# Weight and moving tiles of the second network's matmuls: 64 bytes longer, begun at offsets of 0 to 56 bytes in turn

## The chip, the cores and the metric

The kernel runs on one core of a Trainium2 chip. The metric is the time of one execution on the device in microseconds, the median of repeated runs. TensorE (PE) multiplies a stationary operand (the weights, loaded by a weight load, PEld) with a moving operand that streams past it; VectorE (DVE) and ScalarE (ACT) prepare operands; SyncE (SP) issues the DMAs. All operands of the matmuls lie in the on-chip memory SBUF, which has 128 partitions; a byte address below is the address inside a partition.

## What is computed

An attention between eight blocks of 512 tokens and 32 state rows each, then two feed-forward networks of the same shape, one with a squared ReLU and one with an ELU:

```python
def _moe_ref(x, w_in, w_out):          # 4608 tokens, 512 -> 2048 -> 512
    h = x @ w_in
    r = np.maximum(h, 0.0)
    g = r * r
    return (g @ w_out).astype(np.float32)

def _moe2_ref(x, w_in, w_out):
    h = x @ w_in
    g = np.where(h > 0.0, h, np.exp(np.minimum(h, 0.0)) - 1.0)
    return (g @ w_out).astype(np.float32)

attn_out = _attn_ref(**attn_kwargs)
x = np.ascontiguousarray(attn_out.transpose(0, 2, 1, 3)).reshape(B * S, H * D)
x = _moe_ref(x=x, **moe_kwargs)
return _moe2_ref(x=x, **moe2_kwargs)
```

## The kernel before

Every float32 value is split into a rounded high part and the rest (HI and LO, both of type float32r), and a product of two values is made of three matmuls: HI by LO, HI by HI, LO by HI. `split` makes the two parts: ACT copies the value into HI (L163), DVE subtracts HI from the value and writes LO (L164).

The program has three stretches. In the first (to about 560 us of the span) attention and the first network run block by block; its matmuls are `h<-at,m` and `acc<-gs,v` (L158 to L160), and conversions of the weights of both networks run beside them. In the second (560 to about 687 us) the last two blocks go as a pair. In the third (687 us to the end) the second network runs: four pairs of blocks, one after the other, and then the state rows. A pair is treated as a 2 by 2 block matrix, and the product of two such matrices is made of seven products instead of eight, with sums and differences of the operands as inputs.

In a pair of the second network, `first_product` runs 7 products for each of 8 column groups j, and `second_product` (by way of `out_products`) again 7 products of 8 pieces. Each product of one piece takes one weight tile `wr` (HI and LO, 2 by 256 float32, 2,048 bytes in a partition) and is six matmuls of 512 columns, all on line L43. The moving operand is a tile `xf` (in the first product: HI and LO of 2 by 512 values, 8,192 bytes) or `gp` (in the second: HI and LO of two pieces, 8,192 bytes). `wr` tiles come from HBM by one DMA each (L753), through 12 buffers; `xf` tiles (7 buffers) and `gp` tiles (3 buffers) are written by `split`. Four pairs, two products, 56 pieces, six matmuls: 2,688 matmuls of 512 columns. The state rows follow with 192 matmuls `hs<-xs,pl` and 192 `as<-gss,pl` of 256 columns, whose weights `pl` lie in buffers of the pool `xf`.

Instructions are put into their engines' queues in the order in which the program is written; the background work (`x_forms`, which makes the next pair's `xf`) is called from `second_product` at fixed steps.

Where tiles start is set by the pools, which are laid out one after the other. In the built program of the kernel before, the weight slice and the moving slice of each of the 2,688 and 384 matmuls start at multiples of 64 bytes, and for each matmul the two starts leave the same remainder when divided by 512 (128 and 128, say). The same holds for `acc<-gs,v` and for `x`, `y`, `z<-gp,wr` of the pair of the first network (448 and 448). It does not hold for `h<-at,m`: there the moving slice `at` leaves 448 and the weight slice `m` leaves 128. `h<-at,m` and `X<-xf,wr` are otherwise alike: six matmuls of 512 columns into one bank, in the same order of HI and LO.

Of the kernel before, what the change touches and what calls it, by code (L numbers as in the profile page):

```python
# [10 lines left out]
F32R = mybir.dt.float32r  # L11
# [6 lines left out]
B, H, S, NS, D = 8, 8, 512, 32, 64  # L18
DM, DFF = 512, 2048
P = 128  # L20
# [8 lines left out]
RAW, CV = 4, 4  # L29
NF = 7  # L30
HF = FC // 2

CLAMP = 2.0 ** -96 * (2.0 - 2.0 ** -3 - 2.0 ** -22)
SIGN = -(1 << 31)
# [4 lines left out]
def product(nc, ps, w, x, last, start):  # L39

    for k, (wk, xk) in enumerate(zip(w, x)):
        for i, (a, b) in enumerate(((HI, LO), (HI, HI), (LO, HI))):
            nc.tensor.matmul(ps, wk[a], xk[b], start=start and k == 0 and i == 0,  # L43
                             stop=last and k == len(w) - 1 and i == 2, skip_group_check=True)


def out_products(nc, split, g, weight, unit, step, put, sbuf, psum):


    gp_p, eu_p, u2_p, oo_p = sbuf  # L50
    tt, act = nc.vector.tensor_tensor, nc.scalar.activation
    count = iter(range(NF * HF))

    def phase(f, src, ps, start, combine=None):
        for j in range(HF):
            jj, r = divmod(j, 2)
            if combine and r == 0:
                combine(jj)
            if r % unit == 0:
                t = gp_p.tile([P, 2, unit, S], F32R, name="gp", tag="gp")  # L60
                split(t[:, HI], t[:, LO], src[jj][:, r:r + unit])
            w = weight(j, f)
            for m in range(2):
                sl = slice(m * P, (m + 1) * P)
                product(nc, ps[m], [(w[:, HI, sl], w[:, LO, sl])], [(t[:, HI, r % unit], t[:, LO, r % unit])],
                        j == HF - 1, start and j == 0)
            step(next(count))

    def copied(ps, p, name):
        t = p.tile([P, S], F32, name=name, tag=name)  # L70
        act(out=t, in_=ps, func=AF.Copy)  # L71
        return t

    def added(e, half, ps, u):
        for m in range(2):
            o = oo_p.tile([P, S], F32, name="o", tag="o")
            tt(out=o, in0=ps[m], in1=u[m], op=ALU.add)
            put(e, 2 * half + m, o)

    def sub(out, a, b):  # L80
        return lambda jj: tt(out=out[jj], in0=a[jj], in1=b[jj], op=ALU.subtract)

    a11, a12, a21, a22 = (g[q] for q in (11, 12, 21, 22))
    x, y, z = [[p.tile([P, S], F32, name=c, tag=c) for _ in range(2)] for p, c in zip(psum, "xyz")]
    phase(1, a11, x, True)
    p1 = [copied(t, eu_p, "eu") for t in x]
    phase(2, a12, y, True)
    added(0, 0, y, p1)
    phase(6, a11, x, False, sub(a11, a21, a11))
    u2 = [copied(t, u2_p, "u2") for t in x]  # L90
    phase(5, a21, z, True)
    phase(7, a21, x, False, sub(a21, a22, a11))
    u3 = [copied(t, eu_p, "eu") for t in x]
    added(1, 1, z, u3)
    phase(4, a22, x, False)
    for m in range(2):
        o = oo_p.tile([P, S], F32, name="o", tag="o")
        act(out=o, in_=x[m], func=AF.Copy)
        put(1, m, o)
    phase(3, a12, z, False, sub(a12, a12, a11))  # L100
    added(0, 1, z, u2)
# [3 lines left out]
def attn_mlp_kernel(ctx: ExitStack, tc: tile.TileContext, xt, xn, st, w1, v1, w2, v2, outx, outs):  # L105
# [16 lines left out]
    def pools(stack):  # L122
        return lambda name, bufs, **kw: stack.enter_context(tc.tile_pool(name=name, bufs=bufs, reuse_waits="tile", **kw))

    pool = pools(one)
# [16 lines left out]
    pool = pools(single)  # L142
# [19 lines left out]
    def split(hi, lo, src):  # L162
        copy = nc.scalar.activation(out=hi, in_=src, func=AF.Copy)  # L163
        nc.vector.tensor_tensor(out=lo, in0=src, in1=hi.bitcast(F32), op=ALU.subtract)  # L164
        return copy
# [3 lines left out]
    if True:  # L169
# [30 lines left out]
        def convert(name, i, out):  # L200

            t = raw.pop((name, i))
            low, high = t[:, :, 0], t[:, :, 1]
            bits = out.bitcast(I32)
            after = pace if name in ("w2", "v2") else gate
            with tc.issue_after(after[0].ins) if after else nullcontext():
                nc.scalar.activation(out=out, in_=high.bitcast(F32), func=AF.Copy, scale=2.0 ** -112)  # L210
            with tc.issue_after(gate[0].ins) if gate else nullcontext():
                nc.scalar.activation(out=low, in_=low.bitcast(U32), func=AF.Copy, scale=2.0 ** -29)
            yield
            nc.vector.tensor_scalar(out=out, in0=out, scalar1=CLAMP, scalar2=-CLAMP, op0=ALU.min, op1=ALU.max)
            nc.vector.tensor_single_scalar(out=bits, in_=bits, scalar=3, op=ALU.logical_shift_left)
            yield
            nc.vector.tensor_tensor(out=bits, in0=bits, in1=low, op=ALU.add)
            yield
            nc.vector.scalar_tensor_tensor(out=bits, in0=high, scalar=SIGN, in1=bits, op0=ALU.bitwise_and, op1=ALU.bitwise_or)
# [45 lines left out]
        def conv_pair(name, j):  # L265


            v = [conv_p["cv"].tile([P, 512], F32, name="cv", tag="cv") for _ in range(2)]
            for _ in zip_longest(convert(name, j, v[0]), convert(name, j + HF, v[1])):
                yield  # L270
# [9 lines left out]
        def sums_v1(j):  # L280

            v = [conv_p["cv"].tile([P, 512], F32, name="cv", tag="cv") for _ in range(2)]
            for r in range(2):
                f = j + r * HF
                nc.sync.dma_start(out=v[r], in_=wd["v1", f])
# [11 lines left out]
        for i in range(16):  # L297
            pieces += [("v1", i)] + ([("w1", i + 4)] if i < 12 else [])
        pairs2 = [(name, j) for name in ("w2", "v2") for j in range(HF)]
        converting = pieces + [("f1", j) for j in range(HF)] + pairs2  # L300
# [303 lines left out]
        pool = pools(double)  # L604
# [86 lines left out]
        for i in range(FC + LAG):  # L691
            if i < FC:
# [6 lines left out]
                t = gs[i] = gp1_p.tile([P, 2, NST], F32R, name="gs", tag="gp")  # L699
# [4 lines left out]
            f = i - LAG  # L704
# [4 lines left out]
            w, t = v1s.pop(f), gs.pop(f)  # L709
# [16 lines left out]
    xf_p = pool2("xf", NF)  # L726
    wr_p = pool2("wr", 12)
# [3 lines left out]
    gp_p = pool2("gp", 3)  # L731
# [14 lines left out]
    def copied(ps, p=None, name="eu"):  # L746
        t = (p or eu_p).tile([P, S], F32, name=name, tag=name)
        act(out=t, in_=ps, func=AF.Copy)  # L748
        return t

    def weight(name, j, f):
        t = wr_p.tile([P, 2, 256], F32R, name="wr", tag="wr")
        nc.sync.dma_start(out=t.bitcast(F32), in_=wf[name, j][:, f - 1])  # L753
        return t

    xf, xr = {}, {}
# [5 lines left out]
    def x_forms(n):  # L762

        t1, t2 = xr[2 * n], xr[2 * n + 1]
        a11, a12, a21, a22 = t1[:, DM1], t1[:, DM2], t2[:, DM1], t2[:, DM2]

        def put(f, src):
            t = xf[n, f] = xf_p.tile([P, 2, 2, S], F32R, name=f"xf{n}_{f}", tag="xf")
            split(t[:, HI], t[:, LO], src)

        put(1, a11)
        yield
        put(2, a12)
        yield
        tt(out=a21, in0=a21, in1=a22, op=ALU.add)
        put(5, a21)
        yield
        tt(out=a11, in0=a21, in1=a11, op=ALU.subtract)
        put(6, a11)
        yield  # L780
        tt(out=a21, in0=a22, in1=a11, op=ALU.subtract)
        put(7, a21)
        yield
        put(4, a22)
        yield
        tt(out=a12, in0=a12, in1=a11, op=ALU.subtract)
        put(3, a12)
        yield

    def first_product(n, g):  # L790
# [6 lines left out]
        def prod(f, ps, j, start):  # L797
            w, x = weight("w2", j, f), xf[n, f]
            ws = [(w[:, HI, k * P:(k + 1) * P], w[:, LO, k * P:(k + 1) * P]) for k in range(2)]
            product(nc, ps, ws, [(x[:, HI, k], x[:, LO, k]) for k in range(2)], True, start)  # L800
# [41 lines left out]
    def second_product(n, g, bg):  # L842
        def step(i):
            if i % HF == 3:
                next(bg, None)

        def put(e, k, o):
            nc.sync.dma_start(out=outx[k * P:(k + 1) * P, (2 * n + e) * S:(2 * n + e + 1) * S], in_=o)

        out_products(nc, split, g, lambda j, f: weight("v2", j, f), 2, step, put, (gp_p, eu_p, u2_p, oo_p),  # L850
                     (ps_x, ps_y, ps_z))


    plain = {}
# [3 lines left out]
        nc.sync.dma_start(out=t, in_=wd[name, j])  # L858

    def split_plain(name, j):  # L860
        t = xf_p.tile([P, 2, 2, 512], F32R, name="pl", tag="xf")
        split(t[:, HI], t[:, LO], plain[name, j])
        plain[name, j] = t

# [19 lines left out]
    def state_block(prepared):  # L884
# [5 lines left out]
        def refill():  # L890
            x = next(nxt, None)
            if x:
                split_plain(*x)
            x = next(ahead, None)
            if x:
                load_plain(*x)
# [94 lines left out]
```

## Time and profile before

| | |
|---|---|
| times of the two runs shown | 1352.22 and 1353.41 us, median 1352.82 |
| span of the profiled execution (first to last instruction) | 1350.5 us |
| what lies around the span, by the median | 2.3 us |
| PE busy | 98% of the span, 7,064 matmuls |
| granted TensorE clock, mean | 0.997 |
| third stretch, the four pairs | 687 to 1300 us of the span |
| third stretch, state rows | 1300 us to the end |

The profile gives no time of its own for the profiled execution beside its span. The page's busy shares count each engine's instructions; matmuls are pipelined, so that a matmul's listed length (390 ns) is longer than the distance from its start to the next one's. The pace of PE is read from the chain that ended last, whose pieces are cut where the next one starts: a piece "x48" of 10.88 us is 48 matmuls at 226.7 ns each.

### The profile page before, as it was taken

What the parts mean: (1) busy time and instruction counts of PE and PEld (TensorE: products, weight loads), DVE (VectorE), ACT (ScalarE), POOL (GpSimd) and SP (SyncE); (2) the same over time, 40 slices, a digit from 0 to 9 for tenths busy, and PEclk for the clock granted to TensorE, in tenths of its full rate; (3) what the DMA queues carried; (4) which work ended last, traced back from release to release, by engine and by line L of the source; (5) the groups of instructions that cost most, each with busy time, mean ns of one, the idle gap of its engine ahead of it and who ended that gap; (6) DMA issues with size and microseconds to landing.
All of it is one profiled execution on the core that took longest, in us unless ns stands there. A gap on an engine that the chain in (4) does not pass through costs nothing.

```text
span 1350.5 us, 19746 instructions
## 1 busy us (share of the span) xinstructions
PE 1327.5 (98%) x7064; PEld 1057.1 (78%) x7064; DVE 951.0 (70%) x1437; ACT 839.5 (62%) x1417; POOL 0.7 (0%) x6
## 2 busy tenths in 40 slices
PE   8989999999999999999999999999999999999998
PEld 6656777777777776778988888888888888888898
DVE  6997868686878865775576884579636884568644
ACT  5887758676777657644467843676446743666444
POOL 0000000000000000000000000000000000000000
PEclk9999999999999999999999999999999999999999
DMA  6988856575857424279077777767776777778732
GB/s 240 318 300 310 305 178 230 201 267 190 279 197 266 151 82 153 97 255 349 25 252 208 224 240 224 208 194 247 229 225 194 206 210 223 209 204 284 226 110 100
DMA packets 127729, 290.72 MB, mean 215 GB/s; under 512 B 13840, under 2 KB 22032, under 8 KB 124560
## 3 DMA queue, kind: packets, MB, share of 16 engines
q1 hardware_dynamic: 127632, 289.46, 66.3%
q8 instruction: 56, 0.92, 0.3%
q14 instruction: 41, 0.34, 0.1%
HBM read 212.86 MB, written 76.55 MB: 214 GB/s over the span
## 4 chain that ended last, share of the span: by engine, by line
PE 89%; DMA 5%; DVE 3%; ACT 3%; issue 1%; SPq 0%; ACTq 0%; DVEq 0%
PE x L43 16%; PE X L43 13%; PE z L43 8%; PE Z L43 6%; PE acc L158 6%; PE acc L159 6%; PE acc L160 6%; PE h L158 5%; PE h L159 4%; PE h L160 4%; PE y L43 4%; PE Y L43 3%; DMA raw_v<-in_v_dram 2%; PE mp L331 2%; PE hs L43 2%; PE as L43 2%
## 5 line engine op out<-in xcount | busy, mean ns | idle before, releaser
L163 ACT ACTIVATE gp<-g 128x1024 fp32r<-128x1024 f32 (+1 forms) x168 | 154.0, 917 | 146.0 <-PE x L43 69.5
L164 DVE TENSOR_TENSOR gp<-g,gp 128x1024 fp32r<-128x1024 f32 (+1 forms) x168 | 174.9, 1045 | 95.4 <-ACT gp L163 94.4
L43 PE MATMUL x<-gp,wr 128*128 128x512 f32 x960 | 223.5, 390 | 0.0
L43 PEld LDWEIGHTS x<-gp,wr 128*128 128x128 f32 x960 | 179.7, 188 | 39.4 <-ACT eu L71 1.9
L43 PE MATMUL X<-xf,wr 128*128 128x512 f32 x768 | 186.7, 390 | 0.0
L43 PEld LDWEIGHTS X<-xf,wr 128*128 128x128 f32 x768 | 143.4, 188 | 31.7 <-ACT u L748 1.3
L158 PE MATMUL acc<-gs,v 128*128 128x512 f32 x384 | 154.4, 402 | 3.8 <-DVE gs L474 1.9
L159 PE MATMUL acc<-gs,v 128*128 128x512 f32 x384 | 150.4, 392 | 0.0
L160 PE MATMUL acc<-gs,v 128*128 128x512 f32 x384 | 150.2, 392 | 0.0
L43 PE MATMUL z<-gp,wr 128*128 128x512 f32 x480 | 110.4, 389 | 0.0
L744 DVE SCALAR_TENSOR_TENSOR g<-r,g 128x512 f32<-128x512 f32 x96 | 63.9, 689 | 65.8 <-ACT r L743 65.8
L43 PEld LDWEIGHTS z<-gp,wr 128*128 128x128 f32 x480 | 90.1, 188 | 18.7
L158 PE MATMUL h<-at,m 128*128 128x512 f32 x256 | 103.0, 403 | 1.7 <-ACT r L469 1.7
L158 PEld LDWEIGHTS acc<-gs,v 128*128 128x128 f32 x384 | 72.0, 188 | 38.1 <-issue 15.9
L160 PE MATMUL h<-at,m 128*128 128x512 f32 x256 | 100.7, 395 | 0.5 <-ACT m L346 0.5
L159 PE MATMUL h<-at,m 128*128 128x512 f32 x256 | 101.0, 395 | 0.0
L43 PE MATMUL Z<-xf,wr 128*128 128x512 f32 x384 | 97.4, 389 | 0.0
L469 ACT ACTIVATE r<-h 128x512 f32<-128x512 f32 x96 | 57.1, 595 | 64.4 <-PE h L160 64.1
L742 ACT ACTIVATE r<-g 128x512 f32<-128x512 f32 x96 | 57.5, 625 | 57.5 <-DVE g L821 40.4
L160 PEld LDWEIGHTS acc<-gs,v 128*128 128x128 f32 x384 | 72.1, 188 | 19.8 <-issue 4.2
L159 PEld LDWEIGHTS acc<-gs,v 128*128 128x128 f32 x384 | 72.2, 188 | 18.6 <-issue 3.4
L43 PEld LDWEIGHTS Z<-xf,wr 128*128 128x128 f32 x384 | 72.1, 188 | 15.0
(145 smaller groups left out, 2173.6 us busy)
## 6 DMA issues: line engine op xcount, KB each, us to landing
wr<-f_v SPq DMA_DIRECT2D x256, 256.0 KB, 3.0
wr<-f_w SPq DMA_DIRECT2D x224, 256.0 KB, 2.9
f_v<-wf SPq DMA_DIRECT2D x40, 512.0 KB, 3.3
raw_w<-in_w_dram SPq DMA_DIRECT2D x32, 512.0 KB, 4.8
raw_v<-in_v_dram SPq DMA_DIRECT2D x32, 512.0 KB, 5.0
f_w<-wf SPq DMA_DIRECT2D x24, 512.0 KB, 2.8
xt<-in_xt_dram SPq DMA_DIRECT2D x8, 1024.0 KB, 6.9
xn<-in_xn_dram SPq DMA_DIRECT2D x8, 1024.0 KB, 6.1
```

What stands on the lines that cost most here:

```text
L43: nc.tensor.matmul(ps, wk[a], xk[b], start=start and k == 0 and i == 0, stop=last and k == len(w) - 1 and i == 2, skip_group_check=True)
L158: mm(ps, w[HI], x[LO], start=first, stop=False)
L159: mm(ps, w[HI], x[HI], start=False, stop=False)
L160: mm(ps, w[LO], x[HI], start=False, stop=last)
L163: copy = nc.scalar.activation(out=hi, in_=src, func=AF.Copy)
L164: nc.vector.tensor_tensor(out=lo, in0=src, in1=hi.bitcast(F32), op=ALU.subtract)
L331: mm(ps[e][32 * k:32 * k + 32, :], st_t[b][r, k, :], x(k, r), start=True, stop=True)
L469: pace[:] = [nc.scalar.activation(out=r, in_=ps, func=AF.Relu)]
L742: act(out=r, in_=h, func=AF.Relu, scale=-1.0)
L744: nc.vector.scalar_tensor_tensor(out=out, in0=r, scalar=-1.0, in1=h, op0=ALU.add, op1=ALU.max)
```

## The change

A new function `shifted` makes a tile that is 16 float32 (64 bytes) longer in each partition and returns a view of it that starts `shift` values after the tile's start. Weight tiles `wr` of the second network take their shifts in turn from a list of nine (0, 8, 16, 24, 32, 40, 48, 56 and 4 bytes), tiles `pl` of the state rows from the same list. Moving tiles `xf` and `gp` of the second network take theirs from a list of five (0, 32, 8, 16 and 48 bytes). `gp` of the first network's pair (where `unit` is 1), its weights (`weight1`) and everything before 687 us stay as they are.

```diff
+PAD = 16
+WSHIFT = (0, 2, 4, 6, 8, 10, 12, 14, 1)
+XSHIFT = (0, 8, 2, 4, 12)
...
+def shifted(pool, name, rows, shift):
+
+    n = rows[0] * rows[1] * rows[2]
+    t = pool.tile([P, n + PAD], F32R, name=name, tag=name)
+    return t[:, shift:shift + n].rearrange("p (a b c) -> p a b c", a=rows[0], b=rows[1])
...
-    count = iter(range(NF * HF))
+    count, turn = iter(range(NF * HF)), iter(range(NF * HF))
...
             if r % unit == 0:
-                t = gp_p.tile([P, 2, unit, S], F32R, name="gp", tag="gp")
+                if unit == 1:
+                    t = gp_p.tile([P, 2, unit, S], F32R, name="gp", tag="gp")
+                else:
+                    t = shifted(gp_p, "gp", (2, unit, S), XSHIFT[next(turn) % len(XSHIFT)])
...
+    wturn = iter(range(B * NF * HF))
+
     def weight(name, j, f):
-        t = wr_p.tile([P, 2, 256], F32R, name="wr", tag="wr")
+        t = shifted(wr_p, "wr", (2, 1, 256), WSHIFT[next(wturn) % len(WSHIFT)])[:, :, 0]
         nc.sync.dma_start(out=t.bitcast(F32), in_=wf[name, j][:, f - 1])
...
-            t = xf[n, f] = xf_p.tile([P, 2, 2, S], F32R, name=f"xf{n}_{f}", tag="xf")
+            t = xf[n, f] = shifted(xf_p, "xf", (2, 2, S), XSHIFT[(f + 3 * n) % len(XSHIFT)])
...
-        t = xf_p.tile([P, 2, 2, 512], F32R, name="pl", tag="xf")
+        t = shifted(xf_p, "xf", (2, 2, 512), WSHIFT[len(plain) % len(WSHIFT)])
```

No instruction is added, removed or moved: PE's 6,434, DVE's 1,439, ACT's 1,403 and SP's 867 rows stand in the same order, with the same waits, in the two built programs. Only addresses differ, and the names (`pl` is now called `xf`). Of the 3,072 matmuls of the third stretch, the two starts leave the same remainder by 512 in 42, lie a multiple of 64 bytes apart in 306 and a multiple of 16 bytes apart in 1,230. 1,800 have a weight slice that does not start at a multiple of 16 bytes, and 576 a moving slice that does not; every moving slice starts at a multiple of 8 bytes.

## Rows read from the trace of the kernel before

**Rows 1.** The page: busy us (share) and count of each engine; clock in 40 slices.
```profile
PE 1327.5 (98%) x7064; PEld 1057.1 (78%) x7064; DVE 951.0 (70%) x1437; ACT 839.5 (62%) x1417; POOL 0.7 (0%) x6
...
PEclk9999999999999999999999999999999999999999
```

**Rows 2.** The page, chain that ended last, shares of the span by engine.
```profile
PE 89%; DMA 5%; DVE 3%; ACT 3%; issue 1%; SPq 0%; ACTq 0%; DVEq 0%
```

**Rows 3.** The chain in order of time (first row: second stretch): start us, us, what.
```profile
606.76 10.88 PE x L43 x48
...
775.82 10.88 PE y L43 x48
786.70 10.88 PE x L43 x48
...
845.48 4.08 PE X L43 x18
...
1317.39 2.88 PE hs L43 x24
1320.27 2.88 PE as L43 x24
```

**Rows 4.** The same chain, 526 to 532 us: h, first and last of 22.
```profile
527.07 0.23 PE h L160
...
531.88 0.23 PE h L160
```

**Rows 5.** Stretch 527.07 to 531.88 us: busy us of each engine, clock, DMA share, GB/s.
```profile
527.07:531.88 4.81, 4.81 (x22) 3.78 (x21) 1.98 (x3) 3.42 (x7) 0.00 (x0) 1.00 0.00 0
```

**Rows 6.** The same view, a pair's first product and its second; columns PE, PEld, DVE, ACT, POOL.
```profile
841.30:920.50 79.20, 79.20 (x350) 65.24 (x349) 53.46 (x71) 55.29 (x93) 0.00 (x0) 1.00 0.70 199
920.50:994.20 73.70, 73.69 (x326) 60.70 (x325) 51.22 (x48) 33.96 (x39) 0.00 (x0) 1.00 0.80 243
```

**Rows 7.** Groups by line and shape, 841.3 to 994.2 us: busy us, mean ns | idle before.
```profile
L43 PEld LDWEIGHTS X<-xf,wr 128*128 128x128 f32 x193 | 36.1, 188 | 7.9 <-ACT u L748 0.3 <-ACT eu L748 0.2
L43 PEld LDWEIGHTS x<-gp,wr 128*128 128x128 f32 x192 | 36.0, 188 | 7.9 <-ACT eu L71 0.4
L164 DVE TENSOR_TENSOR gp<-g,gp 128x1024 fp32r<-128x1024 f32 x28 | 34.2, 1223 | 18.4 <-ACT gp L163 18.2
...
L81 DVE TENSOR_TENSOR g<-g,g 128x1024 f32<-128x1024 f32 x12 | 14.6, 1220 | 0.1
...
L163 ACT ACTIVATE gp<-g 128x1024 fp32r<-128x1024 f32 x28 | 29.7, 1059 | 28.5 <-PE x L43 16.0 <-PE z L43 7.3 <-PE y L43 4.0
```

**Rows 8.** Waits of SP's queue, 841.3 to 994.2 us: total us, times, longest.
```profile
SPq L753 <- PE X L43: 30.9, 31, 2.0
SPq L753 <- PE x L43: 23.2, 27, 1.0
```

**Rows 9.** The page, DMA issues: count, KB each, us from issue to landing.
```profile
wr<-f_v SPq DMA_DIRECT2D x256, 256.0 KB, 3.0
wr<-f_w SPq DMA_DIRECT2D x224, 256.0 KB, 2.9
```

## The prediction

> **What bounds the kernel now.** I read the page's first lines, then the chain that ended last, then the stretches. PE is busy 98% of the span and the granted clock is full throughout, its 2.4 GHz level [rows 1]; 89% of the chain is PE [rows 2]. In the third stretch, the only one whose addresses change, the chain is an unbroken row of matmuls at one pace: 48 in 10.88 us and 18 in 4.08 us, 226.7 ns each for 512 columns, and 24 in 2.88 us, 120.0 ns each for 256 columns [rows 3]. The 2,688 matmuls of the four pairs at 226.7 ns are 609.3 us of the 613 us from 687 to 1300. So nothing matters there but this pace: a nanosecond on each of the 2,688 + 384 = 3,072 matmuls is 3.07 us, 0.23% of the time.
>
> What the pace is made of: 512 columns at 2.4 GHz are 213.3 ns and 256 are 106.7 ns, so each matmul has 13.3 ns on top, whatever its length. All these matmuls have their weight and moving starts in step (the same remainder by 512). The one kind that is out of step is h, with starts 320 bytes apart by that measure: from 527.07 to 531.88 us 21 matmuls of 512 columns take 4.81 us, 229.0 ns each [rows 4]. This is 2.4 ns slower, at full clock, with the DMA engines idle [rows 5], and with six matmuls per bank in the same order of HI and LO as X. What is left to tell h from X is where its operands lie. That is one case, and other differences (two writers of the weights instead of a DMA) are not excluded.
>
> **The change part by part.** Order and waits are the same, so the sum has only terms of duration.
>
> 1. The matmul's pace. 42 of 3,072 matmuls stay in step, 3,030 do not. If being out of step costs what it costs in h, that is 3,030 x 2.4 ns = 7.2 us. The bounds: below, the 13.3 ns on top could be something that starts in step bring about; out of step it could shrink to nothing, 3,072 x 13.3 ns = 41 us less. Nothing excludes that, but h, the only row out of step, went the other way. In between lies zero: the pace doesn't care. Above: see the weight loads. I take h's price, as the nearest row, +7.2 us.
>
> 2. The weight loads. One lasts 188 ns and hides beside the running matmul, which leaves 226.7 - 188 = 38.7 ns of slack; the 7.9 us idle before 193 loads are the 41 ns between them [rows 7]. No row shows a load or a matmul whose operand starts off a multiple of 64 bytes. 1,800 of the weight slices will start off a multiple of 16. A load up to 20% longer stays hidden and costs nothing; beyond that each further nanosecond costs 1.8 us. Taken at nothing, with the upper end kept for a rival. For the 576 moving slices off 16 bytes, the same: nothing, or at the far end as much again as the 13.3 ns that a matmul now has on top, 7.7 us.
>
> [...]
>
> 3. The writers of the moving tiles. In a pair's second product ACT is busy 34.0 us and DVE 51.2 us of 73.7 [rows 6]; a `gp` tile takes ACT 1,059 and DVE 1,223 ns [rows 7] and serves 12 matmuls, 2.72 us. If unaligned writes made DVE's share of a tile 10% longer, 0.12 us, it would still be hidden by the three buffers. Nothing. Without that cover (in a phase that combines, a subtraction of 1,220 ns joins the 1,223 ns [rows 7], 2.44 us of work in 2.72) a DVE pace 15% worse would start to show.
>
> 4. The weight DMAs. A tile of 256 KB is needed every 6 x 226.7 ns = 1.36 us, 193 GB/s. A DMA lands 3 us after its issue [rows 9], and 12 buffers reach 16 us ahead; SP waits for PE to free a buffer, not the other way [rows 8]. The DMA engines are 70% busy in a first and 80% in a second product [rows 6]. Unaligned destinations are in no row. Until the packets take 1.25 times as long (1 / 0.80), it costs nothing; I take nothing. Filling the pipe once at 687 us may take some tenths of a microsecond more.
>
> Sum: 7.2 us on the profiled execution's span, 1350.5 to 1357.7 us. 2.3 us lie around the span by the median and don't change, so 1352.8 becomes 1360.0 us, 0.5% slower.
>
> **The rivals.**
>
> *The pace doesn't care where operands start.* Then all of it falls away: 1352.8 us. For it: the pace in rows 3 is the same at remainders of 128 and, in the first network's pair (the piece at 606.76 us), of 448. Against it: h. [...]
>
> *In-step starts are what costs the 13.3 ns.* The running matmul's reads and the next weights' reads could fall on the same part of the memory at the same moments just because all starts are in step; spreading them would then free it. If half of the 13.3 ns goes, 20 us: 1332 us; all of it, 1312 us. For it: the surplus is the same for 256 and 512 columns, as a cost of each weight load would be. Against it: h has other starts and is slower, and a surplus so constant looks like a fixed part of changing weights.
>
> *Unaligned weight slices load slower than they can be hidden* (the other side, beyond the forecast). From 227 ns (now 188) the next matmul waits for its weights. At +30% a load takes 244 ns, 18 ns over the present pace for 1,800 matmuls, 32 us: with the 7 us of the forecast 1392 us. At +50%, 282 ns, 100 us: about 1453 us. For it: the loads are the closest to a limit of all that changes, with 17% of each matmul's time as slack. Against it: nothing but that a pipelined read of 512 bytes has little reason to grow by a third.
>
> *Unaligned DMA destinations bind.* If packets took twice as long, the wr share of the second product's DMA work (56 x 256 KB = 14.7 of some 17.9 MB, 82%) would add 0.66 to 0.80, and a second product would take 1.46 x 73.7 = 107 us, a first one about as long: 60 us more a pair, 1600 us. It decides from 1.25 times. Against it: count and size of the transfers stay the same.
>
> *The change doesn't do what it says*: the built program shows that it does, so no chance is kept for this.
>
> **How the numbers follow.** Chances: h's price, or up to twice it, 0.40; no difference 0.29; starts in step were the cost 0.10 (half of it beyond 2%); slow weight loads, or a moving slice's, 0.15 (0.13 beyond 2%); DMA 0.06. A measurement of this kernel can tell about 2% from no change, 27 us: faster 0.05, slower 0.19, same 0.76. The forecast is 1360 us. The range goes from 1346 (6.7 us below no difference, a third of the half gain of the second rival) to 1392 (a load 30% longer); it leaves out some 0.07 below and 0.12 above.
>
> **What the profile of the changed kernel would show.** The chain's pieces of 48 matmuls: 10.88 us if nothing matters, about 11.0 if h's price holds, 10.3 or less if in-step starts were the cost. If only the slow weight loads bind, the means of the PEld groups on L46 (L43 before) rise above 227 ns and PE waits; if DMAs bind, SP no longer waits for PE at the weight DMA and PE waits for `wr`. ACT and DVE means for `gp` and `xf` should stay at 1,059 and 1,223 ns. The stretch up to 687 us should not move at all. I would be most wrong if a single shift, such as the 4 bytes of every ninth weight tile or the 8 bytes of every fifth moving tile, had a price of a whole different order: then a few of the matmuls would be very slow and the rest unchanged.

## The result and the profile after

The changed kernel takes 1368.41 us (1368.09 to 1368.74) where the kernel before takes 1352.82: a ratio of 1.0111, 95% interval 1.0081 to 1.0140. It is slower, by 15.6 us, inside the forecast range and on the forecast side; the forecast itself, 1360.0, took half of the loss.

The page of the changed kernel, its span and its engines' busy time:

```profile
span 1366.3 us, 19746 instructions
...
PE 1342.0 (98%) x7064; PEld 1057.2 (77%) x7064; DVE 952.5 (70%) x1437; ACT 839.8 (61%) x1417; POOL 0.7 (0%) x6
```

Beside [rows 1], PE is busier by 14.5 us; the weight loads, DVE and ACT are within 1.5 us of where they were. The chain in order of time (start us, us, what; the first row is of the second stretch, whose addresses did not change):

```profile
609.16 10.88 PE x L46 x48
...
779.90 11.20 PE y L46 x48
791.10 11.16 PE x L46 x48
...
1007.60 4.19 PE X L46 x18
...
1333.73 2.86 PE hs L46 x24
```

The first row has the pace of [rows 3], 226.7 ns a matmul, but starts 2.40 us later. In the pairs of the third stretch 48 matmuls take 11.16 to 11.20 us and 18 take 4.19: 232.5 to 233.3 ns, 5.9 to 6.7 more than before. In the state rows, 24 matmuls of 256 columns take 2.86 us in place of 2.88: they are faster.

Three marks in the chains of both kernels divide the loss: the first piece of 18 X, the first piece of hs, and the end. Before, they stand at 691.28, 1299.97 and 1350.5 us:

```profile
691.28 4.19 PE X L43 x18
...
1299.97 9.11 PE hs L43 x76
```

After, the end is at 1366.3 us, and the other two are:

```profile
693.44 4.20 PE X L46 x18
...
1316.44 8.58 PE hs L46 x72
```

Up to the first mark there are 2.16 us more, in code whose addresses are the same, and the row at 609.16 us is already that late. In the experiment with padding alone, whose addresses up to there are the same too, this mark lies at 689.06 us, so executions differ there by as much without any change. The four pairs, 608.69 before, take 623.00: 14.31 us more, 5.3 ns for each of the 2,688 matmuls. The state rows take 0.67 us less. The sum is the 15.8 us by which the span grew.

What the prediction named as other suspects did not move. A first and a second product as in [rows 6] (PE, PEld, DVE, ACT, POOL, clock, DMA share, GB/s), the groups of [rows 7] and the waits of [rows 8]:

```profile
846.00:927.00 81.00, 81.00 (x350) 65.35 (x349) 53.38 (x70) 54.44 (x92) 0.00 (x0) 1.00 0.69 194
927.00:1003.40 76.40, 76.40 (x330) 61.71 (x329) 52.31 (x49) 34.79 (x40) 0.00 (x0) 1.00 0.79 238
```
```profile
L46 PEld LDWEIGHTS x<-gp,wr 128*128 128x128 f32 x192 | 36.1, 188 | 8.8 <-ACT eu L84 0.4
L46 PEld LDWEIGHTS X<-xf,wr 128*128 128x128 f32 x192 | 35.9, 188 | 8.7 <-ACT eu L761 0.2 <-ACT u L761 0.2
L177 DVE TENSOR_TENSOR gp<-g,gp 128x1024 fp32r<-128x1024 f32 x28 | 34.3, 1224 | 20.0 <-ACT gp L176 19.9
L176 ACT ACTIVATE gp<-g 128x1024 fp32r<-128x1024 f32 x28 | 29.6, 1059 | 29.9 <-PE x L46 16.8 <-PE z L46 7.6 <-PE y L46 4.2
```
```profile
SPq L768 <- PE X L46: 31.2, 31, 1.9
SPq L768 <- PE x L46: 25.0, 29, 1.0
```

The clock is full, the share of busy DMA engines is 69 and 79%, a weight load still lasts 188 ns, a `gp` tile still 1,059 and 1,224 ns, and SP still waits for PE. Only the time from one matmul's start to the next has grown, with nothing in the profile that it waits for.

### The profile page after: what moved, and what is told of

The parts are those of the page before. It is cut to its first block, busy times and chain, and to the rows that moved or that the text cites. A ratio compares the mean times of both kernels' runs of the same rounds, so it can differ in the third digit from the quotient of the medians.

```text
span 1366.3 us, 19746 instructions
## 1 busy us (share of the span) xinstructions
PE 1342.0 (98%) x7064; PEld 1057.2 (77%) x7064; DVE 952.5 (70%) x1437; ACT 839.8 (61%) x1417; POOL 0.7 (0%) x6
## 4 chain that ended last, share of the span: by engine, by line
PE 85%; DMA 3%; DVE 2%; ACT 1%; issue 1%; SPq 0%; ACTq 0%; DVEq 0%
PE x L46 16%; PE X L46 13%; PE z L46 8%; PE Z L46 6%; PE acc L171 5%; PE acc L173 5%; PE acc L172 5%; PE h L171 4%; PE h L172 4%; PE h L173 4%; PE y L46 4%; PE Y L46 3%; PE mp L344 2%; PE hs L46 2%; PE as L46 2%; DMA raw_v<-in_v_dram 1%
## 5 line engine op out<-in xcount | busy, mean ns | idle before, releaser
L46 PE MATMUL x<-gp,wr 128*128 128x512 f32 x960 | 227.8, 394 | 0.0
L46 PE MATMUL X<-xf,wr 128*128 128x512 f32 x768 | 190.5, 395 | 0.0
```

## The experiments

Two theories stood at first. STEP: the pace is set by the distance of the weight start from the moving start. UNALIGNED: an operand that starts off some number of bytes costs by itself. A pace below is the mean time from one start to the next over a product or a kind of matmul where no single piece of the chain is quoted, with times over 245 ns (other waits) left out; by this measure the pairs run at 226.8 ns before and 232.3 after; remainders are those of the built program's addresses.

**Padding alone.** The changed kernel with all shifts at zero:

```diff
-WSHIFT = (0, 2, 4, 6, 8, 10, 12, 14, 1)
-XSHIFT = (0, 8, 2, 4, 12)
+WSHIFT = (0,)
+XSHIFT = (0,)
```

> All shifts are zero and only the 64 bytes of padding stay, so every operand starts at a multiple of 64 bytes, but in 2,448 of the 2,688 matmuls of the pairs weight and moving starts leave different remainders by 512 (differences that are multiples of 64). Theory STEP (the pace is set by where the two starts lie relative to each other): as slow as the changed kernel or nearly, pieces of 48 matmuls at 11.0 to 11.2 us, 1362 to 1369 us. Theory UNALIGNED (a start off 64 or 16 bytes costs by itself): pace as before, 10.88 us, 1353 us.

Measured: 1363.32 us, ratio 1.0078 (1.0061 to 1.0095). The chain, pieces of a second product:

```profile
1242.17 11.14 PE y L46 x48
1253.31 11.09 PE x L46 x48
```

So 231 to 232 ns (231.3 over the pairs) with every operand at a multiple of 64 bytes: UNALIGNED alone is out, and the padding, which looks like the harmless part of the change, carries most of the loss, 4.5 of the 5.5 ns. Sorted by distance (remainder by 512 of moving start less weight start; matmuls whose two neighbours have the same distance), the pace of this run is:

```
distance   0     64    128   192   256   320   384   448
pace ns  229.4 230.5 231.8 233.3 229.4 230.6 232.2 233.2
```

The second half repeats the first: what counts is the distance's remainder by 256. By that measure h, at 320, stands at 64, the cheapest of the three distances that are not zero. At distance zero this run has 229.4 ns and not the 226.8 of the kernel before, although both neighbours are at zero as well; why is not shown.

**Both shifted by 8 bytes.** All weight and moving tiles of the pairs in step, all off 16 bytes (edit to the changed kernel):

```diff
-PAD = 16
-WSHIFT = (0, 2, 4, 6, 8, 10, 12, 14, 1)
-XSHIFT = (0, 8, 2, 4, 12)
+PAD = 128
+WSHIFT = (2,)
+XSHIFT = (2,)
```

> Every weight tile and every moving tile of the pairs starts 8 bytes late, with 512 bytes of padding, so that all 2,688 matmuls of the pairs stay in step while none of their operands starts at a multiple of 16 bytes (in the state rows the weights alone are shifted). STEP: pace as before, 10.88 us per 48, 1353 us. UNALIGNED: slower at least as the changed kernel, 11.15 us or more per 48, 1368 us or more.

Measured: 1367.25 us, ratio 1.0110 (1.0089 to 1.0131). The chain:

```profile
784.36 11.09 PE y L46 x48
795.45 11.09 PE x L46 x48
```

231.0 ns in step, 231.9 over the pairs: STEP alone is out as well, though the pieces are a little shorter than the 11.15 us that UNALIGNED asked for. Both things count.

**Weights alone and moving tiles alone,** each through its list, with padding of 512 bytes. The edit to the changed kernel sets `PAD` to 128 and either `XSHIFT` to (0,) or `WSHIFT` to (0,); the other list stays.

> Only the weights are shifted, through the same list of nine; moving tiles start where they started (padding of 512 bytes, so that the shifts are the only differences). 2,388 of 2,688 matmuls are out of step, by 4 to 56 bytes. STEP: slower by most of the changed kernel's 15.6 us, 1362 to 1369 us, if small distances count as large ones do; the 300 in step and the moving operand play no part. UNALIGNED with the weights at fault: 1366 to 1369 us; with the moving operand at fault: 1353 us.

> Only the moving tiles are shifted, through the same list of five (padding of 512 bytes); weights start where they started and none is off 16 bytes. 2,112 of 2,688 matmuls are out of step, by 8 to 48 bytes; the state rows stay as before. STEP: 1361 to 1368 us, and the tiles with shift zero keep 226.7 ns within a piece. UNALIGNED with the moving operand at fault: 1356 us (only 576 are off 16 bytes) to 1368 us; with the weights at fault: 1353 us.

Measured: 1371.32 us, ratio 1.0132 (1.0110 to 1.0154), and 1371.11 us, 1.0137 (1.0122 to 1.0153). The chain of the first, then of the second:

```profile
783.77 11.15 PE y L46 x48
794.92 11.14 PE x L46 x48
```
```profile
784.23 11.13 PE y L46 x48
795.35 11.11 PE x L46 x48
```

Either half of the change has the pace of the whole, 231.5 to 232.3 ns in these pieces and 232.1 over the pairs; the halves don't add. Which of the two operands is shifted makes no difference in the mean, and moving one against the other is enough. Shift by shift they do differ: with the moving tiles alone shifted, products at distance zero ran at 228.6 ns (STEP had asked for 226.7), those at 8, 16, 32 and 48 bytes at 234.4, 231.3, 233.2 and 232.7; with the weights alone shifted, zero ran at 230.0, and the same four shifts at 231.1, 233.4, 233.2 and 233.3. In time both runs lie 3 us above the changed kernel, and above every range expected. That is not their pace, for from the first matmul on `xf` to the first `hs` after the last pair they take 627.5 and 628.6 us, the changed kernel 627.8. In the runs with padding of 512 bytes the third stretch starts later: its first matmul comes 127.3 to 128.4 us after the first of the second stretch, 124.5 in the kernel before and in the changed one; why is not shown. So from here on paces are compared, not times.

**Eight shifts in step, and eight distances.** Each of the eight products has one shift or one distance for all its tiles. The core of the edit, to the kernel before:

```diff
+PAD = 128
+SX, WX = (4, 8, 12, 16), (4, 8, 12, 16)      # sweep of distances: SX (16, 24, 32, 40), WX zero
+SG, WG = (1, 6, 32, 48), (1, 6, 32, 48)      # SG (48, 52, 56, 60), WG zero
...
-        t = wr_p.tile([P, 2, 256], F32R, name="wr", tag="wr")
+        t = shifted(wr_p, "wr", (2, 1, 256), {"w2": WX, "v2": WG}[name][pair_no[0]])[:, :, 0]
...
-            t = xf[n, f] = xf_p.tile([P, 2, 2, S], F32R, name=f"xf{n}_{f}", tag="xf")
+            t = xf[n, f] = shifted(xf_p, "xf", (2, 2, S), SX[n])
```

> All matmuls of the pairs stay in step, and each of the eight products (four pairs, first and second) has its own shift, the same for weights and moving tiles: 16, 32, 48, 64 bytes in the first products, 4, 24, 128, 192 in the second. The run with 8 bytes throughout had 231.9 ns a matmul. Theory BOTH (two things count: the distance of the two starts, and whether a start is a multiple of some number of bytes): 226.7 ns at 64, 128 and 192, 230 to 232 at 4 and 24; at 16, 32 and 48 it tells what the number is, 226.7 at all three if it is 16, at 32 alone if it is 32, at none if it is 64. [...] Rival CHANCE (only one layout happens to be good): 230 ns or more at 64, 128, 192 too.

> Weights start where they started; the moving tiles of each of the eight products start later by one distance that holds for the whole product: 64, 96, 128, 160 bytes in the first products, 192, 208, 224, 240 in the second. In the run with padding alone, where the distance changed from tile to tile, 64 and 320 had 230.6 ns, 128 and 384 had 232.0, 192 and 448 had 233.2, 0 and 256 had 229.4. BOTH with a period of 256 bytes: the same order, 64 at 229 as in h, 128 at 231 to 232, 192 at 233; the three distances off 64 bytes at 231 to 235. A rival (the price comes from changing distances, not from the distance itself): 226.7 at all, or at all multiples of 64.

One execution each: 1365.58 us for the shifts in step, 1374.78 for the distances. In step, the chain's pieces with shifts of 16, 4, 32, 24, 48, 128, 64 and 192 bytes, in this order:

```profile
716.41 4.20 PE X L46 x18
...
782.37 11.41 PE y L46 x48
...
864.68 4.08 PE X L46 x18
...
938.66 11.20 PE y L46 x48
...
1019.99 4.16 PE X L46 x18
...
1094.87 10.88 PE y L46 x48
...
1174.08 4.08 PE X L46 x18
...
1247.69 10.88 PE y L46 x48
```

At 32, 64, 128 and 192 bytes the pace is the old one, 226.7 ns. At 16 and 48 it is 233.3 and 231.1, at 24 and 4 it is 233.3 and 237.7. So the number is 32 bytes, as far as one odd multiple of 32 in one execution can tell; of the outcomes listed it is the middle one. CHANCE is out. Nor do all shifts off 32 bytes cost the same: the cost goes from 4.4 to 11.0 ns, at 4 and 24 bytes to paces above the 230 to 232 ns that BOTH had asked for.

The distances 64, 192, 96, 208, 128, 224, 160 and 240 bytes, in this order:

```profile
717.12 4.12 PE X L46 x18
...
781.99 11.20 PE y L46 x48
...
863.45 4.20 PE X L46 x18
...
939.14 11.26 PE y L46 x48
...
1020.96 4.20 PE X L46 x18
...
1096.60 11.20 PE y L46 x48
...
1178.11 4.22 PE X L46 x18
...
1254.11 11.36 PE y L46 x48
```

A distance that never changes costs about as much as one that does: 228.9 ns at 64 (h's own pace), 233.3 at 96, 128, 192 and 224, 234.4 at 160, 234.6 and 236.7 at 208 and 240, which are also off 32 bytes. Against the table of the run with padding alone, 64 is 1.6 ns cheaper, 128 is 1.5 ns dearer (and above the 231 to 232 expected), and 192 is the same. None of the eight distances is faster than none. Each stands in one product only, the first four in first products and the others in second ones; in the run with padding alone the two kinds differ by at most 1.3 ns at the same distance.

**Who is disturbed: the reads or the writes?** TensorE reads 8 bytes after where the writers write, so that its output is not the network's; a second run has (0, 0) in place of (0, READ). The helper through which `wr`, `xf` and `gp` are made, from the edit to the kernel before (`PAD` 128, `READ` 2):

```diff
+def two_views(nc, pool, name, rows):
+    n = rows[0] * rows[1] * rows[2]
+    t = pool.tile([P, n + PAD], F32R, name=name, tag=name)
+    nc.gpsimd.memset(t[:, n:n + READ].bitcast(F32), 0.0)
+    return [t[:, s:s + n].rearrange("p (a b c) -> p a b c", a=rows[0], b=rows[1]) for s in (0, READ)]
...
```

> In the run with 8 bytes throughout, DMA, ACT and DVE wrote off 32 bytes and TensorE read off 32 bytes. Here all writers write where they wrote in the kernel before (512 bytes of padding), and only TensorE's reads, weights and moving, start 8 bytes later, so that the pairs of the second network multiply columns moved by two and end in two zeroed columns (GpSimd zeroes 8 bytes of each tile). Theory READ (TensorE's own reads set the pace): 231 to 233 ns a matmul, 11.1 us per 48. Rival WRITE (writes off 32 bytes get in the way of the reads): 226.7 ns, 10.88 us per 48.

> The same kernel with TensorE reading where the writers write, so that nothing but the zeroing by GpSimd and the padding of 512 bytes differs from the kernel before. Both theories: 226.7 ns, 10.88 us per 48. If it is slower, the zeroing or the padding costs something and the other run has to be read against this one.

Measured, one time each: 1374.26 and 1356.89 us, the kernel before 1355.34 beside them. The chain with reads at 8, then at 0:

```profile
941.46 11.09 PE y L44 x48
952.55 11.09 PE x L44 x48
```
```profile
933.07 10.88 PE y L44 x48
943.95 10.88 PE x L44 x48
```

11.09 us is to the hundredth the piece of the run where the writes were off as well (over the pairs, 232.2 ns against 231.9). For the shift of 8 bytes, TensorE's own reads set the pace; the writers' offsets add nothing. For the distances no run separates reads from writes; that h pays with the DMA engines idle [rows 5] speaks only against the DMA's writes.

**The layout turned the other way.** Spacers in the kernel before put h in step and give the state rows a distance of 64 or 192 bytes:

```diff
+    pool("gap", 1).tile([P, 48], F32, name="gap", tag="gap")
     xc_p = pool("xc", 2)
...
+    pool2("gap1", 1).tile([P, 16], F32, name="gap1", tag="gap1")
     xf_p = pool2("xf", NF)
...
+    pool2("gap2", 1).tile([P, 48], F32, name="gap2", tag="gap2")
     gq_p = pool2("gq", FC)
+    pool2("gap3", 1).tile([P, 80], F32, name="gap3", tag="gap3")
```

(and shifts of 64 and 192 bytes in the tiles `w1s` and `gs` of the first network's state rows). In the built program the weight start lies 64 bytes after the moving start (`hs`, and `h` of the first network's state rows) or the moving start 192 bytes after the weight start (`as` and `acc`); by the table's measure both are a distance of 192 by 256.

> The kernel before with spacers only: h is put in step (768 matmuls), the pairs stay in step, and the matmuls of 256 columns of both state blocks (2 x 384) get a distance of 64 or 192 bytes, at which the padded run had 113.5 to 116.5 ns in place of 120. BOTH: h at 226.7 in place of 229.4 ns, 2.1 us; the state rows 5 ns less each at the middle of that range, 3.8 us if both blocks gain; together 4 to 7 us less, 1346 to 1349 us where the kernel before has 1352.8, a ratio of 0.995 to 0.997. If the distance is no cause, h keeps 229 ns and the time stays within 0.1%.

Measured: 1349.03 us beside 1353.2, ratio 0.9971 (0.9958 to 0.9984). The chain: seven triples of h from the first to the second row, and the state rows:

```profile
555.71 0.23 PE h L159
...
560.47 0.23 PE h L159
...
1320.58 2.72 PE hs L43 x24
1323.30 2.72 PE as L43 x24
```

Settled, h runs at 4.76 us / 21 = 226.7 ns; its mean over all is 227.5, before 229.4, while `acc<-gs,v`, in step in both kernels, stays at 228.1. The state rows of the second network take 113.3 ns in these pieces in place of 120.0 (means 115.1 for `hs` and 113.4 for `as`); those of the first network come to 117.6 and 115.1. By the means that is 1.4 us for h and 3.6 for the state rows, 5.0 together; the median fell by 4.2, to the upper edge of the times expected. This version beats both kernels, by 0.3% against the kernel before, with an interval that stays below 1.

## Why the prediction was right, and where it was too small

- **The bound** held: the chain is PE's pace before and after, and 14.31 of the 15.8 us lie in the four pairs. The stretch up to 687 us, which should not have moved at all, came 2.2 us later in the profiled execution, with its addresses unchanged.
- **Step 1, the matmul's pace,** had the cause (starts out of step) and the sign right and the size wrong: 2.4 ns taken, 5.3 measured over the pairs and 5.9 to 6.7 in the pieces shown. h was the only row out of step, and its distance (64 by 256) is the cheapest tried at 512 columns: the constant distances from 96 to 240 cost 6.6 to 10 ns. Padding alone, with nothing but distances, brings 4.5 of the 5.5 ns by which the mean pace grew. The 13.3 ns on top follow from the two paces of [rows 3] alone: 256 columns more take 226.7 - 120.0 = 106.7 ns (2.40 columns a nanosecond, the prediction's 2.4 GHz, at a granted clock of 1.00 [rows 6]), and either pace leaves 13.3 ns. That h gave the right sign was partly luck too: in the state rows distances make the matmuls faster.
- **Step 2** took unaligned starts at nothing because no row showed one. In step, a start off 32 bytes costs 4 to 11 ns, not in the weight load (188 to 192 ns by group with 8 bytes throughout, 189 with 4 bytes, 188 before), but in the matmul's pace. In the changed kernel itself this can be no more than a small part: the shifts add 1.0 ns to what the padding costs, and there the 249 matmuls with both starts at multiples of 32 bytes and the 1,173 with neither run alike, at 232.4 ns.
- The term of step 1 priced **the state rows** like the pairs, 0.9 us slower; they became 0.67 us faster. At 256 columns the distances tried make a matmul faster on the whole, not slower.
- **Steps 3 and 4**, the writers and the DMAs, at nothing: right, by the groups and waits above. Filling the pipe at 687 us was no cost either (a DMA piece of 3.50 us where it was 3.74).
- **The rivals.** No difference: out. The loss is a little more than twice the term of 7.2 us, at the edge of what the chance of 0.40 was given to; the part of the range above that was there for slow weight loads, which did not come. Starts in step as the cause of the 13.3 ns: out for 512 columns, where no distance tried is faster than none, and half right for 256, where 120.0 ns became 113.3, half of the surplus. Slow weight loads and bound DMAs: out. That a load above 227 ns makes the next matmul wait was an estimate, which no run shows. The state rows of the kernel before speak against it: the 192 loads for `hs`, 192 ns each, keep PEld busy for 23.6 us, 123 ns a load, so they overlap, and the matmuls still start 120.0 ns apart [rows 3].

```profile
L43 PEld LDWEIGHTS hs<-xs,pl 128*128 128x128 f32 x192 | 23.6, 192 | 0.1
```

That the layout sets the pace is shown, from 226.7 to 237.7 ns for the same instructions; how it does so stays open. Whether reads of the running matmul and of the next weights get in each other's way, as the rival of starts in step supposed, was not shown: no run shows the moment of a stall, and no rule that gives the paces of the distances was found.

## What to carry to other kernels

When the chain is one unbroken row of matmuls, the time from one start to the next, against the columns at the granted clock, is the number to look at, and it can depend on where the operands lie: here, at 512 columns, the best pace measured, 226.7 ns, was reached with starts at multiples of 32 bytes and the same remainder by 512 for weights and moving tiles, and padding of 64 bytes alone brought 231.3. Padding a pool's tiles by anything but a multiple of 512 bytes changes that remainder for tiles after the first, so look up the built addresses before and after. And a price read from the single row that shows an effect is one point of a curve: take it as the forecast if need be, but not as its size.

## What was not expected

- Two layouts of the same instructions differ by up to 11 ns a matmul (226.7 to 237.7), 5%, with weight loads of 188 and 189 ns.
- At 256 columns the best distance is not zero: 113.3 ns at 192 bytes (by 256) against 120.0 in step, in pieces of both `hs` and `as`. For 512 columns 192 bytes costs 6.6 ns.
- In the runs with 512 bytes of padding, which leave every remainder as it was, the third stretch starts some 3 to 4 us later, a fifth to a quarter of the 15.6 us that were to be explained.
